# Sliding-window attention with a GEGLU gate: two chunks of gate/up in turn before their down projections, the last two down projections beside the first heads, and one tile of rows per gate/up block

## The chip, the core and the metric

The kernel runs on one core of a Trainium2 chip. Its engines run beside each other, each with its own queue: TensorE (PE; its weight loads are listed apart as PEld), VectorE (DVE), ScalarE (ACT), GpSimd (POOL), and SyncE (SP), which here only issues transfers. The metric is the device time of one execution in microseconds (us), the median of the runs.

## The reference

With D = 448, 2048 rows, 16 query heads on 8 KV heads of size 256, a window W = 512 of the cache, and F = 1792:

```python
xn = layernorm(x)
q = (xn @ wq) by head
k, v = last 512 rows of the caches, each KV head used by two query heads
s = concat(softmax(q @ k.T * 256**-0.5) @ v) @ wo
g = silu((gelu(xn @ w_gate) * (xn @ w_up)) @ w_down)
out = x + s * g
```

Everything is in bf16 with sums in f32.

## The kernel before

The 2048 rows are four chunks of QC = 512 rows, each of four tiles of 128. Everything stays in SBUF; the order on each engine is the order in which the program calls the operations. A recorder (class Rec) keeps who wrote and who reads each named buffer and puts a semaphore wait where another engine is concerned. When a buffer lies on the place of another, its first use waits for all uses of the old one.

**Start.** Loads are issued on SP: the first chunk's rows, then gate and up weights in four slices (load_gu), with the second chunk's rows (load_x) among them, then the down weights wd and the last two chunks' rows. The first chunk is normalized and transposed on PE into xnT.

**Feed-forward stage**, for each chunk c. gate_up(c, f), f = 0 to 13, is one block: 14 matmuls on PE, where gate and up products of 64 contraction rows each run beside each other, into two PSUM banks; a GELU on ACT from the first bank into hb; a product on DVE of the second bank and hb into actT[f] (line 376). Three pairs of banks go round, so block n + 3 writes what GELU and product n read. In between, the rows of the next chunk are prepared tile by tile: ln_later has statistics and aggregate on DVE and two small operations on POOL (the standard deviation's inverse, rstd, line 347), ln_later2 has two normalizations on DVE (line 294), which wait for rstd, and a transposing transfer on SP (line 236) into xnT. Before the change, ln_later of a tile comes in one block and ln_later2 in the next, so a tile spans two blocks, from block lead on (4 in chunk 0, else 1). The first block of a chunk waits for all four transposes of its rows.

Behind the 14 blocks of chunks 0 to 2 come four down projections (down, line 382): 14 matmuls of 448 columns each, one per actT[f], into bank 6 or 7, and a copy into gy by ACT. Key transposes (kT, on SP) are issued between, and the query, value and output weights (wq, V, wo) come in 22 pieces on POOL's queue (load_piece, line 233), each after the PE operation that precedes it in the program.

**Heads.** q_burst makes the queries of four heads (line 406). Then 16 heads of each of four chunks run, i = 0 to 63, in slots of one row tile, n = 4i + t: scores (line 420, two matmuls, banks 4 and 5), exponential on ACT, reciprocal and scaling on DVE, a transposing transfer on SP of the probabilities into pT (line 236), and from slot 10 on in every second slot values of an earlier head (line 440, four matmuls), from slot 25 on parts of the output projection (line 460). Chunk 3's four down projections are spread as filling over slots 0 to 11 and 16 to 23 (fill), their copies made by DVE (line 389). Buffers of this stage lie on places of the feed-forward stage.

Of the kernel before, what the change touches and what calls it, by code (L numbers as in the profile page):

```python
# [6 lines left out]
ALU = mybir.AluOpType  # L7
BF16 = mybir.dt.bfloat16
# [3 lines left out]
P = 128  # L12
# [129 lines left out]
def bass_recurrent_scan__sliding_block_cached__geglu_ffn__prompt_kernel(nc, A_x, A_k, A_v, A_wq, A_wo, B_x, B_wg, B_wu, B_wd, out):  # L142
    _, S, D = A_x.shape
    Hkv, Sk, Dh = A_k.shape[1], A_k.shape[2], A_k.shape[3]
    HD = A_wq.shape[1]
    Hq = HD // Dh
    W = min(4096, max(256, Sk // 4))
    F = B_wg.shape[1]
    QC, TPC, HP = 512, 4, 64
    NQC = S // QC  # L150
# [8 lines left out]
    with es:  # L159
        off = [16512]  # L160

        def sb(name, shape, dt, at=None):
            n = 4 if dt == F32 else 2
            for x in shape[1:]:
                n *= x
            if at is None:
                at = off[0]
                off[0] += (n + 31) // 32 * 32
            return R.place(name, shape, dt, at), at + (n + 31) // 32 * 32
# [13 lines left out]
        V, _ = sb("V", [P, NJ, Hkv, Dh], BF16)  # L183
        wq, _ = sb("wq", [P, NK, Hkv, Dh], BF16)
        wo, _ = sb("wo", [P, Hq * NE, D], BF16)
        gu_at = off[0]
        wgu, x_at = sb("wgu", [P, NK, F], BF16)
        x4, _ = sb("x4", [P, NT, D], BF16)
# [1 line left out]
        xn2, d_at = sb("xn2", [P, NX, NK, 2, HP], BF16)  # L190
        wd, _ = sb("wd", [P, NF, D], BF16)
        actT, hb_at = sb("actT", [P, NF, QC], BF16)
        NHB = 4
        hb, ffn_end = sb("hb", [P, NHB, QC], BF16)

# [24 lines left out]
        def bank(b, n=512):  # L220
            return psum[:, b * 512:b * 512 + n]
# [10 lines left out]
        def dma(eng, dst, src, w=(), r=(), after=(), lane=None):  # L232
            return R.op(eng, lambda e: e.dma_start(dst, src), r=r, w=w, dma=True, after=after, lane=lane)  # L233

        def dmaT(dst, src, w=(), r=(), after=(), lane=None):
            return R.op("sync", lambda e: e.dma_start_transpose(dst, src), r=r, w=w, dma=True, after=after, lane=lane)
# [22 lines left out]
        def load_x(c):  # L259
            dma("sync", x4[:, c * TPC:(c + 1) * TPC, :], x_view[:, c, :, :],  # L260
                w=[("x4", c * TPC + t) for t in range(TPC)])

        act(lambda e: e.activation(small[:, 2:3], small[:, 0:1], ACT.Sqrt), r=[("eps",)], w=[("warm",)])
        for sl in range(4):
            load_gu(sl)
            if sl == 1:
                load_x(1)
        dma("sync", wd[:, :, :], B_wd.rearrange("(f p) d -> p f d", p=P), w=[("wd",)])
        for c in range(2, NQC):
            load_x(c)  # L270


        v_view = A_v[0, :, Sk - W:Sk, :].rearrange("g (j p) e -> p j g e", p=P)
# [7 lines left out]
        def load_piece():  # L281
            if pieces:
                dst, src, key = pieces.pop(0)
                dma("gpsimd", dst, src, w=[key], after=[R.ops["tensor"][-1]])
# [65 lines left out]
        def ln_later2(t):  # L350
            c, t4 = divmod(t, TPC)
            ln_norm(t)
            dmaT(xnT[:, c, :, t4 * P:(t4 + 1) * P], xn2[:, t % NX, :, :, :].rearrange("p k a d -> p (k a d)"),
                 r=[("xn2", t % NX, 0), ("xn2", t % NX, 1)], w=[("xnT", c, t4)])
# [7 lines left out]
        def gate_up(c, f):  # L362

            n = c * NF + f
            s = 2 * (n % NGB)

            def run(e):
                for k in range(NK):
                    for b, lo in ((s, 0), (s + 1, HP)):
                        ins = e.matmul(bank(b), lhsT=wgu[lo:lo + HP, k, f * P:(f + 1) * P],  # L370
                                       rhs=xnT[lo:lo + HP, c, k, :], start=k == 0, stop=k == NK - 1)
                return ins
            pe(run, r=xn(c) + [("wgu", 0, fslice[f]), ("wgu", 1, fslice[f])], w=[("ps", s), ("ps", s + 1)])
            act(lambda e: e.activation(hb[:, n % NHB, :], bank(s), ACT.Gelu_apprx_tanh),  # L374
                r=[("ps", s)], w=[("hb", n % NHB)])
            dve(lambda e: e.tensor_tensor(actT[:, f, :], bank(s + 1), hb[:, n % NHB, :], ALU.mult),  # L376
                r=[("ps", s + 1), ("hb", n % NHB)], w=[("actT", f)])

        def down(c, t, part=range(NF)):
            b = (6, 7, 7, 2)[t] if c == NQC - 1 else 6 + t % 2  # L380
            for f in part:
                pe(lambda e, f=f: e.matmul(bank(b, D), lhsT=actT[:, f, t * P:(t + 1) * P], rhs=wd[:, f, :],  # L382
                                           start=f == 0, stop=f == NF - 1),
                   r=[("actT", f), ("wd",)], w=[("ps", b)])
            if NF - 1 in part and c < NQC - 1:
                act(lambda e: e.activation(gy[:, c * TPC + t, :], bank(b, D), ACT.Copy),
                    r=[("ps", b)], w=[("gy", c * TPC + t)])
            elif NF - 1 in part:
                dve(lambda e: e.tensor_copy(gy[:, c * TPC + t, :], bank(b, D)),
                    r=[("ps", b)], w=[("gy", c * TPC + t)])  # L390
# [5 lines left out]
        def q_burst(G):  # L396

            c, h0 = divmod(4 * G, Hq)
            for n in range(4):
                hp, e_ = divmod(n, 2)  # L400
                s, i = 2 * (n % 2) if G else (4, 0, 2, 0)[n], (4 * G + 2 * hp) % 6

                def run(e, hp=hp, e_=e_, s=s):
                    for k in range(NK):
                        for b, lo in ((s, 0), (s + 1, HP)):
                            ins = e.matmul(bank(b), lhsT=wq[lo:lo + HP, k, h0 // 2 + hp, e_ * P:(e_ + 1) * P],  # L406
                                           rhs=xnT[lo:lo + HP, c, k, :], start=k == 0, stop=k == NK - 1)
                    return ins
                pe(run, r=xn(c) + [("wq", lo, k) for lo in range(2) for k in range(NK)], w=[("ps", s), ("ps", s + 1)])
                act(lambda e, e_=e_, s=s, i=i: e.activation(  # L410
                    qT[:, i:i + 2, e_, :], psum[:, s * 512:(s + 2) * 512].rearrange("p (a q) -> p a q", a=2), ACT.Copy),
                    r=[("ps", s), ("ps", s + 1)], w=[("qT", i, e_), ("qT", i + 1, e_)])
# [83 lines left out]
        def silu(n):  # L496

            s = n % 2
            act(lambda e: e.activation(tmp[:, s, :], gy[:, n, :], ACT.Tanh, scale=0.5), r=[("gy", n)], w=[("tmp", s)])  # L499
            pool(lambda e: e.tensor_scalar(tmp[:, s, :], tmp[:, s, :], 1.0, 0.5, op0=ALU.add, op1=ALU.mult),  # L500
                 r=[("tmp", s)], w=[("tmp", s)])
            pool(lambda e: e.tensor_tensor(gy[:, n, :], tmp[:, s, :], gy[:, n, :], ALU.mult),
                 r=[("tmp", s), ("gy", n)], w=[("gy", n)])


        for c in range(NQC):
            lead = 4 if c == 0 else 1
            for f in range(NF):
                gate_up(c, f)
                if c + 1 < NQC and lead <= f < lead + 2 * TPC:  # L510
                    t, half = divmod(f - lead, 2)
                    (ln_later2 if half else ln_later)((c + 1) * TPC + t)
                if f >= 9 and f % 2:
                    load_piece()
            for g in ((0, 1), (2, 3, 4), (5, 6, 7), ())[c]:
                for e_ in range(NE):
                    dmaT(kT[:, g, e_, :], A_k[0, g, Sk - W:Sk, e_ * P:(e_ + 1) * P], w=[("kT", g)])
            for t in range(TPC):
                if c < NQC - 1:
                    down(c, t)  # L520
                    load_piece()
        assert not pieces
        act(lambda e: e.activation(small[:, 2:3], small[:, 0:1], ACT.Exp), r=[("eps",)], w=[("warm",)])
        q_burst(0)
        load_xr(0)

        fill = {}
        for d, slots in ((0, range(0, 4)), (1, range(4, 12)), (2, range(16, 20)), (3, range(20, 24))):
            for n, s in enumerate(slots):
                fill[s] = d, range(n * NF // len(slots), (n + 1) * NF // len(slots))  # L530
        pv = [(i, e_) for i in range(NI) for e_ in range(NE)]
        outs = [(G, t) for G in range(NG) for t in range(TPC)]
        for i in range(NI):
            for t in range(TPC):
                scores(i, t)
                if 4 * i + t in fill:
                    down(NQC - 1, *fill[4 * i + t])
                if t % 2 == 0 and 4 * i + t >= 10:
                    values(*pv.pop(0))
                if 6 <= i and t % 2:  # L540
                    outproj(*outs[0], range(2 * t - 2, 2 * t + 2))
                    if t == TPC - 1:
                        outs.pop(0)
                if t == 0 and i % 4 == 3 and i + 1 < NI:
                    q_burst(i // 4 + 1)
            if 7 <= i and (i - 7) % 3 == 0 and (i - 7) // 3 < NT:
                silu((i - 7) // 3)

        for what in "vvovovv":
            if what == "v":  # L550
# [39 lines left out]
```

## Time and profile before

| what | before |
|---|---|
| median of 3 runs | 561.32 us (560.52 to 561.76) |
| the profiled execution | 561.18 us |
| its span | 559.4 us |
| PE busy | 549.0 us (98%) |
| DVE, ACT, POOL busy | 322.9, 296.1, 90.1 us |
| gate/up matmuls (line 370) | 784, 85.5 us |
| down matmuls (line 382) | 224, 46.2 us |
| products (line 376), each | 685 ns |
| normalizations (line 294), each | 501 ns |
| row statistics (line 288), each | 614 ns |

A line of the chain or of the timeline begins with its start and its length in us, then engine, line, operation, and written and read buffers; the bracket at its end is the idle time before it and what ended that. Lines that merge several instructions give their number as xN. Matmuls are pipelined: one of 512 columns is listed with 376 to 379 ns from start to end, while two gate and up matmuls together pass in about 0.22 us.

### The profile page before, as it was taken

What the parts mean: (1) busy time and instruction counts of PE and PEld (TensorE: products, weight loads), DVE (VectorE), ACT (ScalarE), POOL (GpSimd) and SP (SyncE); (2) the same over time, 40 slices, a digit from 0 to 9 for tenths busy, and PEclk for the clock granted to TensorE, in tenths of its full rate; (3) what the DMA queues carried; (4) which work ended last, traced back from release to release, by engine and by line L of the source; (5) the groups of instructions that cost most, each with busy time, mean ns of one, the idle gap of its engine ahead of it and who ended that gap; (6) DMA issues with size and microseconds to landing.
All of it is one profiled execution on the core that took longest, in us unless ns stands there. A gap on an engine that the chain in (4) does not pass through costs nothing.

```text
span 559.4 us, 9865 instructions
## 1 busy us (share of the span) xinstructions
PE 549.0 (98%) x3499; PEld 257.2 (46%) x3532; DVE 322.9 (58%) x835; ACT 296.1 (53%) x673; POOL 90.1 (16%) x125
## 2 busy tenths in 40 slices
PE   7999999999999999999999999999999999999997
PEld 3544444444444444444444444444444444444445
DVE  5636446143464847474846657484747484755674
ACT  4324233247655565556565656656565656565641
POOL 0232323200000111013501101232100021400023
PEclk9999999999999999999999999999999999999999
DMA  8994746972453435353664344445535353645352
GB/s 193 276 191 86 138 102 136 247 137 65 94 85 68 97 64 99 69 91 64 143 98 94 73 86 71 81 84 137 101 67 99 63 95 71 147 79 101 70 92 52
DMA packets 169552, 58.83 MB, mean 105 GB/s; under 512 B 160160, under 2 KB 166432, under 8 KB 169504
## 3 DMA queue, kind: packets, MB, share of 16 engines
q1 hardware_dynamic: 166208, 45.50, 44.2%
q0 software_dynamic: 3152, 12.65, 8.9%
q8 instruction: 28, 0.46, 0.4%
q14 instruction: 20, 0.16, 0.1%
q10 hardware_dynamic: 144, 0.06, 0.0%
HBM read 17.92 MB, written 1.84 MB: 35 GB/s over the span
## 4 chain that ended last, share of the span: by engine, by line
PE 95%; DMA 1%; DVE 1%; issue 1%; SPq 1%; ACT 0%
PE ps L440 20%; PE ps L420 19%; PE ps L406 18%; PE ps L460 16%; PE ps L370 15%; PE ps L382 8%; DMA wgu<-in_B_w_up_dram 1%; SPq L233 1%; DVE tmp L469 0%; DVE ofin L471 0%; DVE pr L427 0%; DVE oT L446 0%; DVE rden L426 0%; ACT pr L424 0%
## 5 line engine op out<-in xcount | busy, mean ns | idle before, releaser
L424 ACT ACTIVATE pr<-ps 128x512 bf16<-128x512 f32 x256 | 152.8, 597 | 116.6 <-PE ps L420 112.5
L420 PE MATMUL ps<-kT,qT 128*128 128x512 bf16 x481 | 145.4, 379 | 3.3 <-issue 2.5
L440 PE MATMUL ps<-pT,V 128*128 128x512 bf16 x510 | 130.8, 379 | 0.6 <-DVE rden L426 0.4
L426 DVE RECIPROCAL rden<-den 128x1 f32<-128x1 f32 x256 | 41.5, 162 | 152.4 <-ACT pr L424 134.3
L460 PE MATMUL ps<-wo,oT 128*128 128x448 bf16 (+1 forms) x536 | 116.3, 344 | 0.0
L427 DVE TENSOR_SCALAR pr<-pr,rden 128x512 bf16<-128x512 bf16 x256 | 106.4, 416 | 9.0
L406 PE MATMUL ps<-xnT,wq 64*128 64x512 bf16 x896 | 99.5, 376 | 0.0
L410 ACT ACTIVATE qT<-ps 128x1024 bf16<-128x1024 f32 x64 | 65.5, 1024 | 49.8 <-PE ps L406 49.8
L370 PE MATMUL ps<-xnT,wgu 64*128 64x512 bf16 x784 | 85.5, 376 | 1.0 <-ACT xnT L322 0.8
L446 DVE CAST oT<-ps 128x512 bf16<-128x512 f32 x124 | 84.6, 682 | 0.6 <-PE ps L440 0.5
L440 PEld LDWEIGHTS ps<-pT,V 128*128 128x128 bf16 x512 | 49.9, 98 | 60.8 <-issue 1.2
L460 PEld LDWEIGHTS ps<-wo,oT 128*128 128x128 bf16 x536 | 52.3, 98 | 51.1
L420 PEld LDWEIGHTS ps<-kT,qT 128*128 128x128 bf16 x512 | 48.5, 98 | 57.1 <-issue 7.3
L376 DVE TENSOR_TENSOR actT<-ps,hb 128x512 bf16<-128x512 f32 x56 | 38.1, 685 | 57.5 <-ACT hb L374 55.7
L406 PEld LDWEIGHTS ps<-xnT,wq 64*128 64x128 bf16 x896 | 42.4, 94 | 55.9 <-DVE acc L481 4.2
L374 ACT ACTIVATE hb<-ps 128x512 bf16<-128x512 f32 x56 | 33.4, 597 | 51.8 <-PE ps L370 51.8
L370 PEld LDWEIGHTS ps<-xnT,wgu 64*128 64x128 bf16 x784 | 39.2, 94 | 46.5 <-issue 2.5
L424 ACT ACTIVATION_READ_ACCUMULATOR pr<-ps 128x1 f32 x256 | 49.9, 195 | 0.0
L500 POOL TENSOR_SCALAR tmp<-tmp 128x448 f32<-128x448 f32 x16 | 9.1, 572 | 233.9 <-ACT tmp L499 233.9
L382 PE MATMUL ps<-wd,actT 128*128 128x448 bf16 x224 | 46.2, 353 | 0.1
L485 POOL TENSOR_TENSOR tmp<-acc,gy 128x448 f32<-128x448 f32 x16 | 16.6, 1035 | 123.2 <-DVE acc L481 123.2
L382 PEld LDWEIGHTS ps<-wd,actT 128*128 128x128 bf16 x224 | 21.7, 98 | 22.2 <-issue 1.3
(43 smaller groups left out, 171.7 us busy)
## 6 DMA issues: line engine op xcount, KB each, us to landing
pT<-pr SPq DMA_TRANSPOSE x256, 2.4
wq<-in_A_wq_dram POOLq DMA_DIRECT2D x14, 256.0 KB, 4.3
wo<-in_A_wo_dram POOLq DMA_DIRECT2D x4, 896.0 KB, 10.1
V<-in_A_v_cache_dram POOLq DMA_DIRECT2D x4, 512.0 KB, 5.8
xr<-in_A_x_dram POOLq DMA_DIRECT2D x4, 448.0 KB, 4.8
wd<-in_B_w_down_dram SPq DMA_DIRECT2D x1, 1568.0 KB, 17.6
wgu<-in_B_w_gate_dram SPq DMA_DIRECT2D x3, 448.0 KB, 10.3
wgu<-in_B_w_up_dram SPq DMA_DIRECT2D x3, 448.0 KB, 11.8
```

Of the source, the lines that this page charges most:

```text
L370: ins = e.matmul(bank(b), lhsT=wgu[lo:lo + HP, k, f * P:(f + 1) * P], rhs=xnT[lo:lo + HP, c, k, :], start=k == 0, stop=k == NK - 1)
L376: dve(lambda e: e.tensor_tensor(actT[:, f, :], bank(s + 1), hb[:, n % NHB, :], ALU.mult), r=[("ps", s + 1), ("hb", n % NHB)], w=[("actT", f)])
L382: pe(lambda e, f=f: e.matmul(bank(b, D), lhsT=actT[:, f, t * P:(t + 1) * P], rhs=wd[:, f, :], start=f == 0, stop=f == NF - 1), r=[("actT", ...
L406: ins = e.matmul(bank(b), lhsT=wq[lo:lo + HP, k, h0 // 2 + hp, e_ * P:(e_ + 1) * P], rhs=xnT[lo:lo + HP, c, k, :], start=k == 0, stop=k == ...
L410: act(lambda e, e_=e_, s=s, i=i: e.activation(qT[:, i:i + 2, e_, :], psum[:, s * 512:(s + 2) * 512].rearrange("p (a q) -> p a q", a=2), AC ...
L420: ins = e.matmul(bank(b), lhsT=qT[:, i % 6, k, t * P:(t + 1) * P], rhs=kT[:, g, k, :], start=k == 0, stop=k == NE - 1)
L424: act(lambda e: e.activation(pr[s][:, :], bank(b), ACT.Exp, scale=scale, accum_out=den[:, s:s + 1]), r=[("ps", b)], w=[("pr%d" % s,), ("de ...
L426: dve(lambda e: e.reciprocal(rden[:, s:s + 1], den[:, s:s + 1]), r=[("den", s)], w=[("rden", s)])
L427: dve(lambda e: e.tensor_scalar(pr[s][:, :], pr[s][:, :], rden[:, s:s + 1], None, op0=ALU.mult), r=[("pr%d" % s,), ("rden", s)], w=[("pr%d ...
L440: ins = e.matmul(bank(b), lhsT=V[:, j, g, e_ * P:(e_ + 1) * P], rhs=pT[:, i % NPT, j, :], start=j == 0, stop=j == NJ - 1)
L446: dve(lambda e: e.tensor_copy(dst, bank(b)), r=[("ps", b)], w=[key])
L460: ins = e.matmul(bank(b, D)[:, lo:hi], lhsT=oT[G % 2][:, idx, t * P:(t + 1) * P], rhs=wo[:, h0 * NE + idx, lo:hi], start=idx == 0, stop=id ...
```

## The change

The loop over chunks runs gate/up of chunks 0 and 1, then the down projections of both (eight), then gate/up of chunks 2 and 3. The down projections of chunks 2 and 3 (eight) are the filling of slots 0 to 15, half of one per slot, behind the slot's other matmuls. Two actT buffers serve in turn: actT for chunks 0 and 3, actB for 1 and 2. actB lies on the first half of wo's place, so wo's four pieces are issued in slots 9, 11, 13 and 15. The copies of chunk 2's down projections go from ACT to DVE.

In the blocks, ln_later2 of a tile and ln_later of the next stand in the same block, so a tile takes one block, and four tiles take five blocks in place of eight. The loads of wd and of the last rows go behind chunk 0's blocks on SP, the first key transposes behind chunk 1's. Weight pieces begin in chunk 1: one in blocks 3, 7 and 11 of each chunk, one at each of the eight down projections, and the rest of V before the heads.

```diff
+        actB, _ = sb("actB", [P, NF, QC], BF16, off[0] - Hq * NE * D * 2)
...
+        ffn = [("actT", actT), ("actB", actB), ("actB", actB), ("actT", actT)]
...
-        dma("sync", wd[:, :, :], B_wd.rearrange("(f p) d -> p f d", p=P), w=[("wd",)])
-        for c in range(2, NQC):
-            load_x(c)
+        load_x(2)
+
+        def load_wd():
+            dma("sync", wd[:, :, :], B_wd.rearrange("(f p) d -> p f d", p=P), w=[("wd",)])
...
-            b = (6, 7, 7, 2)[t] if c == NQC - 1 else 6 + t % 2
+            b = ((6, 7, 6, 7), (6, 7, 7, 3))[c - 2][t] if c >= 2 else 6 + t % 2
+            name, buf = ffn[c]
...
-            if NF - 1 in part and c < NQC - 1:
+            if NF - 1 in part and c < 2:
                 act(lambda e: e.activation(gy[:, c * TPC + t, :], bank(b, D), ACT.Copy),
...
+        def load_kT(heads):
+            for g in heads:
+                for e_ in range(NE):
+                    dmaT(kT[:, g, e_, :], A_k[0, g, Sk - W:Sk, e_ * P:(e_ + 1) * P], w=[("kT", g)])
+
         for c in range(NQC):
             lead = 4 if c == 0 else 1
             for f in range(NF):
                 gate_up(c, f)
-                if c + 1 < NQC and lead <= f < lead + 2 * TPC:
-                    t, half = divmod(f - lead, 2)
-                    (ln_later2 if half else ln_later)((c + 1) * TPC + t)
-                if f >= 9 and f % 2:
+                if c + 1 < NQC and lead < f <= lead + TPC:
+                    ln_later2((c + 1) * TPC + f - lead - 1)
+                if c + 1 < NQC and lead <= f < lead + TPC:
+                    ln_later((c + 1) * TPC + f - lead)
+                if c and f % 4 == 3:
                     load_piece()
-            for g in ((0, 1), (2, 3, 4), (5, 6, 7), ())[c]:
-                for e_ in range(NE):
-                    dmaT(kT[:, g, e_, :], A_k[0, g, Sk - W:Sk, e_ * P:(e_ + 1) * P], w=[("kT", g)])
-            for t in range(TPC):
-                if c < NQC - 1:
-                    down(c, t)
-                    load_piece()
-        assert not pieces
+            if c == 0:
+                load_wd()
+                load_x(3)
+            else:
+                load_kT(((), (0, 1), (2, 3, 4), (5, 6, 7))[c])
+            if c == 1:
+                for a in range(2):
+                    for t in range(TPC):
+                        down(a, t)
+                        load_piece()
+        while len(pieces) > Hq * NE // 8:
+            load_piece()
...
-        for d, slots in ((0, range(0, 4)), (1, range(4, 12)), (2, range(16, 20)), (3, range(20, 24))):
-            for n, s in enumerate(slots):
-                fill[s] = d, range(n * NF // len(slots), (n + 1) * NF // len(slots))
+        for d in range(2 * TPC):
+            for n in range(2):
+                fill[2 * d + n] = NQC - 2 + d // TPC, d % TPC, range(n * NF // 2, (n + 1) * NF // 2)
...
                 scores(i, t)
-                if 4 * i + t in fill:
-                    down(NQC - 1, *fill[4 * i + t])
...
+                n = 4 * i + t
+                if n in fill:
+                    down(*fill[n])
+                    if n > 2 * TPC and n % 2:
+                        load_piece()
```

More of the change, by code (lines that the diff above doesn't have):

```diff
@@ L375, in gate_up @@
                 r=[("ps", s)], w=[("hb", n % NHB)])
-            dve(lambda e: e.tensor_tensor(actT[:, f, :], bank(s + 1), hb[:, n % NHB, :], ALU.mult),
-                r=[("ps", s + 1), ("hb", n % NHB)], w=[("actT", f)])
+            name, buf = ffn[c]
+            dve(lambda e: e.tensor_tensor(buf[:, f, :], bank(s + 1), hb[:, n % NHB, :], ALU.mult),
+                r=[("ps", s + 1), ("hb", n % NHB)], w=[(name, f)])
         def down(c, t, part=range(NF)):
-            b = (6, 7, 7, 2)[t] if c == NQC - 1 else 6 + t % 2
+            b = ((6, 7, 6, 7), (6, 7, 7, 3))[c - 2][t] if c >= 2 else 6 + t % 2
+            name, buf = ffn[c]
             for f in part:
-                pe(lambda e, f=f: e.matmul(bank(b, D), lhsT=actT[:, f, t * P:(t + 1) * P], rhs=wd[:, f, :],
+                pe(lambda e, f=f: e.matmul(bank(b, D), lhsT=buf[:, f, t * P:(t + 1) * P], rhs=wd[:, f, :],
                                            start=f == 0, stop=f == NF - 1),
-                   r=[("actT", f), ("wd",)], w=[("ps", b)])
-            if NF - 1 in part and c < NQC - 1:
+                   r=[(name, f), ("wd",)], w=[("ps", b)])
+            if NF - 1 in part and c < 2:
                 act(lambda e: e.activation(gy[:, c * TPC + t, :], bank(b, D), ACT.Copy),
@@ L545, in bass_recurrent_scan__sliding_block_cached__geglu_ffn__prompt_kernel @@
                     q_burst(i // 4 + 1)
+                n = 4 * i + t
[3 more added lines that the diff above has]
+                        load_piece()
             if 7 <= i and (i - 7) % 3 == 0 and (i - 7) // 3 < NT:
                 silu((i - 7) // 3)
+        assert not pieces
         for what in "vvovovv":
```

## The prediction

> **What bounds the kernel now.** I read the summary first: TensorE (PE) is busy 549.0 of 559.4 us at the full granted clock, so only a change in PE's waits can move the time.
>
> ```profile
> span 559.4 us, 9865 instructions
> PE 549.0 (98%) x3499; PEld 257.2 (46%) x3532; DVE 322.9 (58%) x835; ACT 296.1 (53%) x673; POOL 90.1 (16%) x125
> PEclk9999999999999999999999999999999999999999
> ```
>
> Second, the chain that ended last, in order of time. In the feed-forward stage it is PE alone, block after block: 14 gate/up blocks take 21.26 us (1.52 each), 56 down matmuls 10.70, a query burst 6.04.
>
> ```profile
> 30.98 10.70 PE ps L382 x56
> 41.68 21.26 PE ps L370 x196
> 62.94 10.70 PE ps L382 x56
> 73.64 21.26 PE ps L370 x196
> 94.89 10.70 PE ps L382 x56
> 105.59 21.26 PE ps L370 x196
> 126.85 6.04 PE ps L406 x56
> ```
>
> Each stretch begins where the last ends: here no wait is left to remove. Third, VectorE (DVE) in order of time beside chunk 1's blocks, since the change moves row work onto it there.
>
> ```profile
> 47.06 0.69 DVE L376 TENSOR_TENSOR actT<-ps,hb 128x512 bf16<-128x512 f32 x1
> 48.05 0.92 DVE L294 TENSOR_SCALAR xn<-x,mv,rstd 128x448 bf16<-128x448 bf16 x2 [0.30 <-POOL rstd L347]
> 48.89 0.68 DVE L376 TENSOR_TENSOR actT<-ps,hb 128x512 bf16<-128x512 f32 x1
> 49.49 0.62 DVE L288 BATCH_NORM_STATS2 stats<-x 128x6 f32<-128x448 bf16 x1
> 50.14 0.18 DVE L289 BATCH_NORM_AGGREGATE mv<-stats 128x2 f32<-128x6 f32 x1
> 50.24 0.67 DVE L376 TENSOR_TENSOR actT<-ps,hb 128x512 bf16<-128x512 f32 x1
> 51.38 0.92 DVE L294 TENSOR_SCALAR xn<-x,mv,rstd 128x448 bf16<-128x448 bf16 x2 [0.47 <-POOL rstd L347]
> 52.22 0.68 DVE L376 TENSOR_TENSOR actT<-ps,hb 128x512 bf16<-128x512 f32 x1
> ```
>
> Start to start: product to statistics 0.60, statistics to aggregate 0.65, aggregate to product 0.10, product to normalization 1.14 (0.47 of it a wait for POOL's rstd; the normalization comes 1.24 after its aggregate), two normalizations to product 0.84. A row tile with its two products takes the sum, 3.33 us, in two blocks, while PE needs 3.02. DVE is slightly too slow already; the backlog of four tiles, about 1.2 us, fits into the three pairs of PSUM banks. Matmul rows of that stretch show no wait.
>
> **The change, part by part. (1) A whole tile per block.** One block's DVE order becomes product, two normalizations of the last tile, statistics and aggregate of the next: 1.14 + 0.84 + 0.65 + 0.10 = 2.73 us, against PE's 1.51. Laid on the times of chunk 1 above (blocks 0 to 13, lead 1): product 2 starts at 47.06 as now and its normalization at 48.05; then statistics 48.88, aggregate 49.53, product 3 at 49.63, product 4 at 52.36 (+2.73), product 5 at 55.09 (+2.73), the last normalization 56.23, product 6 at 57.07. Without backlog product 6 would start at 47.06 + 4 x 1.51 = 53.10: it is 3.97 late. A block may write its two banks only when gelu and product of three blocks before are through. GELUs start at 52.40 (block 6), 53.91 (7) and 55.42 (8), each 0.1 after its block's end. So block 7, free to start at 52.30, waits for product 4 to end (52.36 + 0.69 = 53.05): 0.8 us. Block 8 would start at 54.6 and waits for product 5, 55.78: 1.2. Block 9 would start at 57.35 and waits for product 6, 57.76: 0.5. In all block 9 starts at 57.8 instead of 55.32: 2.49 us lost. After that only products remain, 0.60 apart, and DVE catches up. The same sums on chunk 0 (lead 4, product 5 at 19.63) put product 9 at 29.65 and block 12 at 30.39 instead of 27.90, again 2.49; chunk 2's rows have the same spacing as chunk 1's. Chunk 3 has no tiles. **3 x 2.49 = +7.5 us**, all on PE. POOL's two small operations keep their 1.24; the weight piece queued behind the third tile waits for a PE block finished long before, and its issue (0.68 to 0.92) ends before the next aggregate, 2.73 later.
>
> **(2) Chunk 1 at once after chunk 0.** The 10.70 us of down matmuls that stood before its first block are gone. That block needs all four transposed tiles. Chunk 0 ends at 30.92 + 2.49 = 33.4; the last normalization runs 28.82 to 29.74, and its transpose must land by 33.4. Landing took 7.3 us in that place, behind the down weights and two row loads on the same queue, and 2.9 where the queue was free.
>
> ```profile
> xnT<-xn SPq DMA_TRANSPOSE x1, 7.3
> ```
> ```profile
> xnT<-xn SPq DMA_TRANSPOSE x1, 2.9
> ```
>
> (Issues between 30.5 and 34, then between 51.5 and 54 us.) The change takes the down weights (1.57 MB) and the last row load (0.46 MB) from before the transposes, and the query weight pieces out of chunk 0; only the third row load stays, done about 25 by the 0.22 to 0.34 MB/us moved there. I take 2.9: lands at 32.6, 0.8 early, cost 0. Bounds 0 and 7.3 - (33.4 - 29.74) = 3.6. If it were late, gate/up of chunk 1 would be, and nothing could fill in. Chunks 2 to 3: the last normalization ends 8 us before chunk 2 does; 5.2, the longest landing there, fits.
>
> **(3) Loads moved on SP and POOL, at 0.** Down weights issue after that transpose (about 31; issue 2.73, landing at most 17.6: 49) and are used at 33.4 + 23.75 = 57. Row load 3 is needed at 81. The key transposes of KV heads 2 to 4 stand behind chunk 2's last row transpose on SP, those of 5 to 7 right behind them, with nothing to wait for: 12 at 2.6 each (five took 12.91) after about 96 end at 127, and SP's first probability transpose comes at 131. Without that cover it would be late by the rest, and values, ten slots on, would not notice. Of the 14 query weight pieces (0.71 us of POOL each) the last goes in chunk 2, 25 us before the burst. The last V piece (lands in 5.8) is issued beside the burst and used ten slots, 17 us, later.
>
> **(4) Down projections of chunk 2 into the heads.** 56 x 0.19 = 10.7 us leave the stage and 10.5 arrive (four matmuls 0.75): -0.2. Their four evacuations go from ScalarE (0.54) to DVE (0.62); slots 0 to 15 cost PE 0.43 + 7 x 0.1875 = 1.75 us and DVE under 1.2, so these are covered; without the cover it would be 4 x 0.62. Slots 0 to 23 now take 33.3 us, against 33.0 of matmuls (24 x 0.43, seven values of 0.86, burst 6.14, 56 downs), so more filling can win 0.3 at most. Slots 16 to 23 lose their filling and fall to (2 x 0.43 + 0.86)/2 = 0.86; the slots that now run at 0.75 show no PE wait.
>
> **(5) Output weights loaded beside the heads.** wo's four pieces (0.92 MB each) wait for the fills of slots 9, 11, 13 and 15, because actB lies on their place. Counting from slot 0's scores, the last two are issued at 32.4 and 36.7 us. The probabilities of slot 15 are ready for their transpose at 36.9, those of slot 19 at 41.7 (1.2 us of SP each); values need them at 42.3 (slot 22) and 46.5 (slot 26). So landings up to 5.4 and 4.8 cost nothing. They take 2.5 now; key transposes of this size took 4.7 beside wq pieces and 7.1 beside V and wo. Bounds 0 and 7.1 - 4.8 = +2.3; I take 5.3, nearer to the first row as two pieces in 12 us are less traffic: +0.5. The software queue can shut the other out: between 40 and 42 us one had everything, with a key transpose outstanding.
>
> ```profile
> q0 software_dynamic: 112, 0.39, 106.1%
> ```
>
> The Trainium skill (DMA: Bandwidth & Descriptors, Queues, rings and completion order) says instead that each DMA engine takes turns between its queues packet by packet. By that a transpose would at worst about double, to 5.0, and this term would be +0.2. The row, where turns did not come for 2 us, speaks for more.
>
> **Sum.** The profiled execution took 561.18 (span 559.40 and 1.8 around it; the median is 561.32). 561.2 + 7.5 + 0 + 0 - 0.2 - 0.1 (of the 0.3) + 0.5 = **568.9**.
>
> **Rivals. (a) The banks absorb it: 560.9, not slower.** If the four blocks' DVE work took at most 7.5 us instead of 10.0 (1.9 per block), product 6 would be at most 1.5 late, which the three bank pairs cover, and only -0.2 and -0.1 were left. For it: today's backlog of 1.2 costs nothing. Against it: even without the four waits for rstd (4 x 0.47) 8.1 remain.
> **(b) Chunk 1's rows land late.** If the landing stays at 7.3, PE waits up to 3.6 us more: 572.5. For it: the third row load still precedes; against: the 2.03 MB before it are gone. The trace grants the clock at 1.00 in every stretch, but it has no PE wait of this length after the start. The Trainium skill (TensorE: Matmul & The Clock Gate, Part 1) lets the clock fall to half after an idle window of about 3.4 us: this one wait would reach that, and 1.7 us more would be an estimate from that page.
> **(c) wo against the transposes** at its upper bound: 568.9 + 1.8 = 570.7, more if both slots wait.
>
> **How the numbers follow.** Forecast 66% (its own range 567.8 to 570.2), (a) or something near it 10%, (b) in part or whole 12%, (c) 12%. About 0.2%, 1.1 us, is what a measurement here can tell from no change. Faster 0.04 and same 0.05 come from (a), slower 0.91. Low 566.0 leaves out (a) and holds a stall a third smaller; high 572.5 holds (c) and nearly all of (b).
>
> **What would show it.** DVE's products beside blocks lead+2 to lead+4 start 2.73 apart; the gate/up matmuls show waits for the DVE product at three blocks in each of the chunks 0, 1, 2 and in none of chunk 3; those stretches take 23.75 instead of 21.26. Chunk 1's first block shows no wait for a transpose. wo lands during slots 10 to 20; a values matmul that waits for DMA would be (c). If the gate/up stretches stay at 21.3, step 1 is wrong and with it the forecast.

## The result and the profile after

The changed kernel takes 568.88 us (median of 4 runs, 568.51 to 570.24) against 561.34 for the kernel before, run four times beside it: 1.0142 times the time, 95% interval 1.013 to 1.0155. Its profiled execution took 568.51, with a span of 566.7 us, 7.3 more than before.

The summary of the page, and its group of the gate/up matmuls (busy us and mean ns, then the idle time of PE just before them and what ended most of it):

```profile
span 566.7 us, 9871 instructions
PE 550.6 (97%) x3498; PEld 261.6 (46%) x3532; DVE 326.5 (58%) x839; ACT 293.9 (52%) x669; POOL 90.0 (16%) x125
L374 PE MATMUL ps<-xnT,wgu 64*128 64x512 bf16 x784 | 86.8, 376 | 7.1 <-DVE actB L381 4.3
```

PE's work is the same; it is the idle time that grew. The same matmuls had 1.0 us of it before, none from DVE. PE in order of time, chunk 1 from its block 7 on:

```profile
44.85 1.69 PE L374 MATMUL ps<-xnT,wgu 64*128 64x512 bf16 x14 [0.81 <-DVE actB L381]
47.58 1.69 PE L374 MATMUL ps<-xnT,wgu 64*128 64x512 bf16 x14 [1.03 <-DVE actB L381]
49.57 7.73 PE L374 MATMUL ps<-xnT,wgu 64*128 64x512 bf16 x70 [0.30 <-DVE actB L381]
```

Three blocks, 7, 8 and 9, wait for a product of DVE. The idle times begin at the modelled end of the last matmul, about 0.15 after the next could have started. By starts (blocks 1.52 apart when nothing waits) the three cost 2.59 us. DVE in the same stretch:

```profile
41.31 0.67 DVE L381 TENSOR_TENSOR actB<-ps,hb 128x512 bf16<-128x512 f32 x1
42.45 0.92 DVE L298 TENSOR_SCALAR xn<-x,mv,rstd 128x448 bf16<-128x448 bf16 x2 [0.47 <-POOL rstd L351]
43.29 0.62 DVE L292 BATCH_NORM_STATS2 stats<-x 128x6 f32<-128x448 bf16 x1
43.94 0.18 DVE L293 BATCH_NORM_AGGREGATE mv<-stats 128x2 f32<-128x6 f32 x1
44.04 0.67 DVE L381 TENSOR_TENSOR actB<-ps,hb 128x512 bf16<-128x512 f32 x1
```

Products 2.73 us apart, with the wait for rstd still in each block; before, two products and one tile shared 3.33. In chunk 0 the three waits stand at blocks 10 to 12; there the profile puts the first down to issue and the other two to the product. Chunk 3, which has no tiles to prepare, shows no such wait: in the chain that ended last, one piece of 19 blocks holds the last five of chunk 2 and all 14 of chunk 3.

```profile
94.80 28.88 PE ps L374 x266
123.69 6.04 PE ps L412 x56
```

By stage, from those starts: chunk 2's blocks take 23.84 us (21.26 before), the query burst starts 3.16 earlier than before with four down projections (10.70) less ahead of it, so 7.54 were lost by then. From that burst to the third one (start 180.40, 172.78 before) 56.71 us pass in place of 45.93, which is 10.78 for 10.5 to 10.7 of matmuls. The rest takes 386.3 in place of 386.6. One wait is new in the heads, in slot 26:

```profile
176.89 1.02 PE L446 MATMUL ps<-pT,V 128*128 128x512 bf16 x4 [0.30 <-DMA pT<-pr]
```

### The profile page after: what moved, and what is told of

The parts are those of the page before. It is cut to its first block, busy times and chain, and to the rows that moved or that the text cites. A ratio compares the mean times of both kernels' runs of the same rounds, so it can differ in the third digit from the quotient of the medians.

```text
span 566.7 us, 9871 instructions
## 1 busy us (share of the span) xinstructions
PE 550.6 (97%) x3498; PEld 261.6 (46%) x3532; DVE 326.5 (58%) x839; ACT 293.9 (52%) x669; POOL 90.0 (16%) x125
## 4 chain that ended last, share of the span: by engine, by line
PE 88%; DVE 6%; issue 2%; POOL 2%; DMA 1%; ACT 1%; DVEq 0%; ACTq 0%
PE ps L446 19%; PE ps L426 18%; PE ps L412 17%; PE ps L466 16%; PE ps L374 10%; PE ps L388 8%; DVE xn L298 2%; DVE stats L292 2%; POOL rstd L351 1%; DMA pT<-pr 1%; DVE mv L293 1%; POOL std L349 0%; DVE actB L381 0%; DVE tmp L475 0%; DVE ofin L477 0%
## 5 line engine op out<-in xcount | busy, mean ns | idle before, releaser
L374 PE MATMUL ps<-xnT,wgu 64*128 64x512 bf16 x784 | 86.8, 376 | 7.1 <-DVE actB L381 4.3
L374 PEld LDWEIGHTS ps<-xnT,wgu 64*128 64x128 bf16 x784 | 42.6, 94 | 50.8 <-ACT hb L378 7.1
L381 DVE TENSOR_TENSOR actB<-ps,hb 128x512 bf16<-128x512 f32 x28 | 19.0, 686 | 34.0 <-ACT hb L378 33.0
L381 DVE TENSOR_TENSOR actT<-ps,hb 128x512 bf16<-128x512 f32 x28 | 19.2, 689 | 19.6 <-ACT hb L378 19.5
L487 DVE TENSOR_TENSOR acc<-ps,acc 128x448 f32<-128x448 f32 x44 | 27.2, 617 | 3.3 <-PE ps L466 3.3
```

Source lines behind the costliest of these rows:

```text
L381: dve(lambda e: e.tensor_tensor(buf[:, f, :], bank(s + 1), hb[:, n % NHB, :], ALU.mult), r=[("ps", s + 1), ("hb", n % NHB)], w=[(name, f)])
```

## The experiments

Theory A is that of the prediction: a whole row tile per block makes DVE's products late, and the block three later waits for its banks. The rivals: B, the chunk order and the moved loads cost the time; C, the loss is DVE's amount of work and does not go through the wait for rstd or the banks. Each ratio below is to the kernel before, timed again beside the run (560.96 to 561.62 us).

**One part alone.** The kernel before, with only the tile per block:

```diff
-                if c + 1 < NQC and lead <= f < lead + 2 * TPC:
-                    t, half = divmod(f - lead, 2)
-                    (ln_later2 if half else ln_later)((c + 1) * TPC + t)
+                if c + 1 < NQC and lead < f <= lead + TPC:
+                    ln_later2((c + 1) * TPC + f - lead - 1)
+                if c + 1 < NQC and lead <= f < lead + TPC:
+                    ln_later((c + 1) * TPC + f - lead)
```

> The kernel before with one part of the change alone: a row tile per block, five blocks in place of eight. Theory A: PE waits for DVE's product before blocks lead+6 to lead+8 in chunks 0, 1, 2, 2.5 us each, so 561.3 + 7.5 = 568.8, as slow as the whole change. Rival B: 561.3, since the down projections stand between the chunks and DVE catches up there.

Measured 569.27 us, ratio 1.0133 (1.0115 to 1.0151). PE in order of time, chunk 1:

```profile
55.99 1.69 PE L370 MATMUL ps<-xnT,wgu 64*128 64x512 bf16 x14 [0.81 <-DVE actT L376]
58.72 1.69 PE L370 MATMUL ps<-xnT,wgu 64*128 64x512 bf16 x14 [1.04 <-DVE actT L376]
60.70 7.73 PE L370 MATMUL ps<-xnT,wgu 64*128 64x512 bf16 x70 [0.30 <-DVE actT L376]
```

The same three waits of the same size. This part is the loss, whatever the order of the chunks.

**That part undone.** The changed kernel with the two-block form (the removed lines above, in place of the added ones):

> The changed kernel with its row tiles spread over two blocks each again (statistics in one block, normalization in the next, eight blocks per chunk); chunk order, moved loads and the filling of the heads stay. Theory A (DVE's tile per block costs 2.5 us in each of three chunks): the three waits of PE for DVE's products go, 7.5 us. But chunk 0's last normalization then ends about 31.4 us, its transpose lands 2.9 later, and chunk 1 wants its rows at 30.7: about 3.5 us of waiting for the transpose, and 0 to 1.1 more between chunks 2 and 3. So 564.9 to 566. Rival B (the order of the chunks and the moved loads cost the time, the tiles per block do not): 568.9 or more.

Measured 568.23 us (565.47 to 568.54), ratio 1.0101 (1.0068 to 1.0134): as a median neither theory's number. No wait for a product is left. But chunk 1's rows come late, as expected, and then something follows that I had not counted. PE in order of time, the whole of chunk 1:

```profile
34.47 24.21 PE L374 MATMUL ps<-xnT,wgu 64*128 64x512 bf16 x196 [3.87 <-DMA xnT<-xn]
```

and stretches of a microsecond (window, length, busy us and instructions of PE, its weight loads, DVE, ACT, POOL, then PE's granted clock, DMA share and GB/s):

```profile
33.00:34.00 1.00, 0.00 (x0) 0.00 (x0) 0.00 (x0) 0.00 (x0) 0.00 (x0) 0.76 0.93 123
35.00:36.00 1.00, 1.00 (x8) 0.36 (x5) 0.00 (x0) 0.00 (x0) 0.00 (x0) 0.50 0.99 318
```

After about 3 us of idleness the granted clock falls to half and stays there to about 40 us: the chunk takes 24.21 in place of 21.3. The wait cost 3.9 and its consequence 2.9. The other executions agree: three of the four list a mean granted clock of 0.993 to 0.996 and took 568.1 to 568.5; the one at 1.000 took 565.47, inside theory A's range.

To take that second cause away, the tiles of chunk 0 start at block 1 in place of 4:

```diff
-            lead = 4 if c == 0 else 1
+            lead = 1
```

> The two-blocks kernel again, its row tiles in chunk 0 from block 1 on in place of block 4 (the rows land about 14.2 us). Theory A (the tile per block is all of the loss; what was left in the two-blocks run came from chunk 1's last transpose, 3.9 us of waiting and then 2.9 us at half clock): the last normalization of chunk 0 ends about 26.9, its transpose lands 2.9 to 4.7 later, before or up to 1 us after chunk 1 wants it at 30.6. No wait, no drop of the clock: 561.3, the time of the kernel before, at most 562.3. Rival B (the order of the chunks costs something by itself): 565 or more, as in the two-blocks run.

Measured 562.12 us, ratio 1.0023 (1.0009 to 1.0037). Chunk 1 starts without a wait. What remains in the chunks of its profile is one wait of 1.75 us before chunk 3, the place where the first form had expected 0 to 1.1:

```profile
96.99 21.33 PE L374 MATMUL ps<-xnT,wgu 64*128 64x512 bf16 x196 [1.75 <-DVE actB L381]
```

The last transpose, issued at 91.3, took 5.4 to land, with key transposes right behind it and query weight pieces on the other queue. (The profile puts that wait down to a product; it ended by chance at the same moment, and block 0 does not need it.) Rival B falls: order, loads and filling together cost about 1 us. The profiled execution, at 563.46, is one of the slower ones, so how much of that 1 us is this wait stays open.

**The wait for rstd.** Same work of DVE, but each normalization two blocks behind its statistics:

```diff
-                if c + 1 < NQC and lead < f <= lead + TPC:
-                    ln_later2((c + 1) * TPC + f - lead - 1)
+                if c + 1 < NQC and lead + 2 <= f < lead + 2 + TPC:
+                    ln_later2((c + 1) * TPC + f - lead - 2)
```

> The changed kernel with each tile's normalization two blocks behind its statistics in place of one, so that rstd is there when DVE gets to it. DVE's work is the same, only its wait for POOL goes, and no more than two blocks hold both halves of a tile. Theory A: a full block takes DVE 0.60 + 0.84 + 0.65 + 0.10 = 2.19 us in place of 2.73, two of them put the products 1.36 us late at most, less than the 1.5 that three bank pairs cover: no wait in the blocks. Chunk 0's last transpose is issued about 28.2 and lands 31.1, 0.4 after chunk 1 wants it. 568.9 - 7.5 + 0.4 = 561.8. Rival C (DVE's amount of work in the chunks sets the loss, not the wait for rstd and the place in the blocks): 568.9, or 567 if only the 0.5 of each wait is saved.

Measured 563.64 us (562.6 to 565.55), ratio 1.004 (1.0023 to 1.0056). All waits for products are gone; rival C falls: the amount of work alone does not cost the time. The run changes two things at once, though, since the same work now spreads over six blocks with both halves of a tile in only two of them; the wait for rstd was not removed by itself. What lies over the expectation is again chunk 1's last transpose and the clock: in the profiled execution it took 4.5 to land, with the down weights issued right behind it, in place of the 2.9 taken; PE waited 2.3 us, and half clock from 34.0 to 37.4 added 1.7. The first line is PE in order of time, the others are stretches as above:

```profile
33.15 23.06 PE L374 MATMUL ps<-xnT,wgu 64*128 64x512 bf16 x196 [2.29 <-DMA xnT<-xn]
```
```profile
33.00:34.00 1.00, 0.85 (x8) 0.48 (x10) 0.00 (x0) 0.00 (x0) 0.00 (x0) 1.00 1.05 330
34.00:35.00 1.00, 1.00 (x8) 0.52 (x6) 0.00 (x0) 0.00 (x0) 0.00 (x0) 0.51 1.08 339
37.00:38.00 1.00, 1.00 (x10) 0.53 (x8) 0.00 (x0) 0.00 (x0) 0.00 (x0) 0.78 1.05 392
```

The clock falls when PE has been at work again for 0.9 us, some 3.2 after it stopped. This profiled execution took 564.99; of the nine, three list a mean clock of 0.997 or less (564.9 to 565.55), and the six at 0.999 to 1.000 took 562.6 to 564.94, so the drop does not come every time.

With chunk 0's tiles from block 2 on (lead 2 in place of 4):

> The lag-two kernel with its row tiles in chunk 0 from block 2 on, wo's pieces in slots 9 to 15 as in the changed kernel. Theory A: neither chunk 1's transposes nor the clock cost anything any more, only slot 26 does: 560.15 of the kernel with the later pieces + 0.4 = 560.5. If the early start of the tiles is not what removed the 2.3 us wait and the half clock behind it, 563.6 as in the lag-two run.

Measured 561.24 us, ratio 0.9997 (0.998 to 1.0014). No wait for transposed rows, full clock throughout; slot 26 waited 1.3 us in its profile. Its wo pieces are moved in the last pair below.

**The banks.** Four pairs in place of three:

```diff
-        NGB = 3
+        NGB = 4
...
-            b = ((6, 7, 6, 7), (6, 7, 7, 3))[c - 2][t] if c >= 2 else 6 + t % 2
+            b = ((6, 7, 6, 7), (6, 7, 7, 3))[c - 2][t] if c >= 2 else 2 + t % 2
```

> The changed kernel with four pairs of PSUM banks for the gate/up blocks in place of three (the first eight down projections use banks 2 and 3). DVE's schedule is untouched. Theory A: the products are as late as before, 3.97 us, but a block needs the banks of four blocks before, so 1.5 us more are covered: 1.0 us of waiting per chunk in place of 2.5, 568.9 - 4.5 = 564.4. Rival C: the loss does not go through the banks, 568.9.

Measured 567.78 us, ratio 1.011 (1.0082 to 1.0138): a miss. The waits for products did shrink, from 2.1 listed in chunk 1 to 0.8 to 0.9 in each chunk (about 1.1 by starts, 1.0 expected), but the blocks of chunk 0 ended earlier, and chunk 1's transpose, which took 4.7 to land this time, was waited for: 2.6 us, and 1.7 more at half clock from 35.0 to 38.4.

```profile
34.42 15.46 PE L374 MATMUL ps<-xnT,wgu 64*128 64x512 bf16 x126 [2.62 <-DMA xnT<-xn]
```
```profile
35.00:36.00 1.00, 1.00 (x9) 0.36 (x5) 0.00 (x0) 0.00 (x0) 0.00 (x0) 0.50 1.08 335
```

Two of the four executions list a mean clock of 0.997 (568.55, the profiled one, and 569.43), the other two 1.000 (566.36 and 567.01). With chunk 0's tiles from block 2 on:

> The four-pairs kernel again, its row tiles in chunk 0 from block 2 on in place of block 4. Theory A: PE's waits for the products stay at 0.8 to 0.9 us per chunk as in the four-pairs run, the 2.6 us of waiting for chunk 1's last transpose and the 1.7 us at half clock behind it go. 568.9 - 7.5 + 2.6 = 564.0. Rival C (more banks win nothing): 567.8 or more.

Measured 564.51 us (564.31 to 564.59), ratio 1.0066 (1.0052 to 1.008). Its profile shows DVE's backlog meeting one more pair; PE, chunk 1, blocks 9 and 10:

```profile
46.55 1.69 PE L374 MATMUL ps<-xnT,wgu 64*128 64x512 bf16 x14 [0.51 <-DVE actB L381]
48.55 6.22 PE L374 MATMUL ps<-xnT,wgu 64*128 64x512 bf16 x56 [0.31 <-DVE actB L381]
```

So the loss goes through the banks, as the sum had it.

**The moved loads.** The down weights and both late row loads again on SP ahead of chunk 1's transposes:

```diff
-        load_x(2)
+        dma("sync", wd[:, :, :], B_wd.rearrange("(f p) d -> p f d", p=P), w=[("wd",)])
+        for c in range(2, NQC):
+            load_x(c)
...
-            if c == 0:
-                load_wd()
-                load_x(3)
-            else:
+            if c:
                 load_kT(((), (0, 1), (2, 3, 4), (5, 6, 7))[c])
```

> The changed kernel with the down weights and the last two row loads on SP ahead of chunk 1's transposes again, as before the change. Theory A: those loads drain about 28 us, the four transposes behind them follow, the last lands at 33 to 34 where PE wants it at 33.0: 0 to 1 us, so 568.9 to 569.9. Rival (b) of the prediction (the landing stays at 7.3 us): it lands at 36.9, 3.8 us of waiting and, as the two-blocks run showed, about 2.9 more at half clock: 575.

Measured 571.94 us (570.44 to 573.43), ratio 1.0204 (1.0182 to 1.0226), between the two. The last transpose took 4.7 to land, and chunk 1 waited (the profile puts it down to a product that ended late; the block needs only much earlier ones):

```profile
35.66 10.75 PE L373 MATMUL ps<-xnT,wgu 64*128 64x512 bf16 x98 [1.53 <-DVE actT L380]
```

The stretches around and behind its start, with the granted clock third from the end:

```profile
35.00:37.00 2.00, 1.33 (x14) 0.74 (x16) 0.57 (x1) 0.00 (x0) 0.00 (x0) 1.00 0.00 0
37.00:40.00 3.00, 3.00 (x32) 1.55 (x30) 1.09 (x2) 1.19 (x2) 0.00 (x0) 1.00 0.00 0
```

In this execution (571.05) the clock was granted at 1.00 all through, so this wait of 1.5 us did not bring it down. Of the other three, which left no trace, two list a mean clock of 0.997 (572.83 and 573.43), as the profiled execution of the lag by two blocks did with its 3.4 us at half clock: there too it probably fell, behind a wait of unknown length. Moving the loads was worth about 3 us by the medians; rival (b) of the prediction was real, at a smaller size in the profile.

**wo beside the transposes.** Three of its pieces later, into slots 29, 45 and 61:

```diff
-                    if n > 2 * TPC and n % 2:
-                        load_piece()
+                if n in (9, 29, 45, 61):
+                    load_piece()
```

> The changed kernel with three of wo's four pieces issued in slots 29, 45 and 61 in place of 11, 13 and 15. Theory (c) at its size in the profile of the changed kernel: values in slot 26 waited 0.3 to 0.5 us for a transpose of probabilities, which took 4.3 to 5.8 us to land beside wo and 2.5 without; that wait goes, the landings in slots 12 to 20 fall to 2.5: 568.5, of the 568.9. Rival: wo costs nothing, the wait at slot 26 comes from SP, which issues a transpose every 1.2 us while slots 16 to 23 last 0.86: the wait stays and so do 568.9.

Measured 568.22 us (567.95 to 568.38), ratio 1.0122 (1.0109 to 1.0136). The wait of slot 26 is gone, and from the first to the third burst 56.26 us pass in place of 56.71. Landings of the probabilities issued between 165 and 170 us, changed kernel first, then this one (us at the end):

```profile
pT<-pr SPq DMA_TRANSPOSE x4, 5.6
```
```profile
pT<-pr SPq DMA_TRANSPOSE x4, 2.4
```

SP's pace was the same in both, so it was wo that held the transposes.

**All of it together**, normalizations two blocks behind, chunk 0's tiles from block 2, wo later:

> The lag-two kernel with its row tiles in chunk 0 from block 2 on, and with three of wo's four pieces issued later (slots 29, 45 and 61 in place of 11, 13 and 15). Theory A: no wait for products, none for chunk 1's transposes (issued about 25, landing by 30), none at slot 26. 568.9 - 7.5 - 0.4 = 561.0, level with the kernel before, whose PE had nothing to win either. A gain of more than 0.5 us over before would show a wait in before that I have not seen.

Measured 560.15 us (559.93 to 560.34), ratio 0.9983 (0.9974 to 0.9991), the fastest of all, ahead of the kernel before by 0.8 us. That is more than the 0.5 at which the expectation wanted an unseen wait in the kernel before. By starts in the two profiles about 0.2 of it lies ahead of the first burst, 0.35 between the first and third, where the filling is, and 0.25 behind; no single wait was found for it. From block 2 of chunk 0 on PE does not wait in the chunks; its timeline from there to the end of chunk 1 is one piece of 26 blocks:

```profile
12.70 39.55 PE L374 MATMUL ps<-xnT,wgu 64*128 64x512 bf16 x364 [0.20 <-DMA wgu<-in_B_w_up_dram]
```

and DVE there does not wait for POOL:

```profile
40.60 0.91 DVE L298 TENSOR_SCALAR xn<-x,mv,rstd 128x448 bf16<-128x448 bf16 x2
```

## Why the prediction was right, point by point

**(1) A tile per block, +7.5: right in mechanism and size.** The steps came out as written: products 2.73 apart, waits at three blocks per chunk, none in chunk 3. The three stretches lost 2.4 (chunk 0), 2.59 and 2.58 us against 2.49 each. Alone in the old kernel the part costs the whole loss; without the wait for rstd, and over six blocks in place of five, DVE does the same work at no loss (the two were not tried apart; by the sum of rival (a), 8.1 us without the waits against 7.5 covered, the wait alone would not have sufficed); one more pair of banks leaves about 1.1 of each 2.6, where the sum had 1.0. The sum worked because it was laid on starts, not on busy times: DVE is busy 58% of the span, and nothing in that share shows that five blocks in a row are over-full.

**(2) Chunk 1's rows, 0: right, on thin cover.** The last transpose landed in the 2.9 taken, in the profiled execution. But with the down weights right behind it, as here, it also took 4.5 (normalizations two blocks behind) and 4.7 (four pairs). The kernel with wo later issues it at the same time as the one with four pairs, with the same transfers behind it, and there it took 2.9. The margin was 0.8, so at 4.7 chunk 1 would have waited about 1 us, an estimate from these numbers: that it cost nothing was in part luck. My bounds treated 2.9 and 7.3 as two states of a queue and left out the landings in between.

**Rival (b)'s consequence was right in kind and low in size.** In the profiles the drop followed waits of 2.3, 2.6 and 3.9 us and cost 1.7, 1.7 and 2.9; a wait of 1.5 did not bring it, nor did the three shorter ones per chunk of the changed kernel. The half clock lasted 3.4 us twice and 6.8 once, and set in 2.9 to 3.2 us after PE had stopped, in two of the three when it was at work again. The Trainium skill (TensorE: Matmul & The Clock Gate, Part 1) has the clock fall to half after an idle window of about 3.4 us, from which I gave 1.7 us for a wait that long. The lengths measured here, 3.4 and twice 3.4, fit that window as a unit. Its threshold did not hold here: an idle time of 2.3 us was enough.

**(3) Moved loads and pieces, 0: right.** Nothing waits for the down weights (landed in 8.7 in place of 17.6), the key transposes, V or the query weights.

**(4) Filling, -0.2 and -0.1.** The stretch to the third burst grew by 10.78, the wait at slot 26 included, against 10.8 to 10.9 forecast. With wo out of the way 45.56 us plus the 10.70 moved there show what filling wins: 45.93 - 45.56 = 0.4, where the two terms together were 0.3 (0.5 with the second at its bound).

**(5) wo, +0.5: right in place and mechanism.** Landings were 4.3 to 5.8 (5.3 taken), the wait came in slot 26, at 0.3 as listed and 0.45 by starts. Its size is not steady: about 0.3 to 1.3 in the variants with the same pieces. The turn-taking rule of the Trainium skill (DMA: Bandwidth & Descriptors, Queues, rings and completion order) that I weighed against the row gave +0.2 and landings of 5.0 at worst; with 0.45 and landings up to 5.8 (the median of one stretch) the row was nearer.

**The sum** was 568.9 against 568.88, closer than its terms deserve: the profiled execution lost 7.3 where 7.7 was the sum, since the heads up to the third burst cost 0.1 and not 0.2, and those after it ran 0.3 faster. Every kernel with the new filling is 0.1 to 0.35 faster there; I did not settle why.

## What to carry to other kernels

An engine at 58% busy can still set the time where its work is packed: lay its starts on the bottleneck's blocks, add the waits inside the block, and compare the backlog with what the buffers between the two engines cover. Work that depends on a slower helper need not wait out its latency if it is placed further behind the request: two blocks of distance in place of one, with the work spread over one block more, took every wait for a product away here. And a removed neighbour stage is also cover for what ran beside it; whoever closes the gap has to start the next stage's inputs earlier.

## What I had not expected

PE's idle time has a price beyond itself. A wait of 2.3 us for a transfer cost 1.7 more because the granted clock went to 0.50 for 3.4 us, and one of 3.9 cost 2.9 more; in the one profile with 1.5 it cost nothing more. And the same transposing transfer, alone in its queue when issued, landed in 2.9 us or in 4.5 to 5.4. The long ones had further transfers issued right behind them, but so had some of 2.9; what decides between the two was not found.
